# Sinkhorn attention with a bilinear feed-forward: batch 0's q in full width during Sinkhorn

## The chip, the cores and the metric

The kernel runs on one core of one Trainium2 chip. The metric is the device time of one execution in microseconds (us); before the change the median of 7 runs is 251.01 us (250.98 to 251.25). The engines are named as in the profile: PE (matrix multiply; PEld its weight loads), DVE (vector), ACT (scalar), POOL (GpSimd, which also issues the loads from memory), SP (issues the other DMAs).

## The reference

Inputs are q, k, v of 4 batches x 8 heads x 768 positions x 64 and an 8 x 8 `sort_net` per head; the weights `w_a`, `w_b` are 512 x 1536 and `w_out` 1536 x 512. All are float32.

```python
P = sort_net                                  # Sinkhorn, 5 rounds
for _ in range(5):
    P = np.exp(P - P.max(-1, keepdims=True))
    P = P / (P.sum(-1, keepdims=True) + 1e-9)
    P = P / (P.sum(-2, keepdims=True) + 1e-9)
k_sorted = einsum('bhij,bhjcd->bhicd', P, k_blocks)   # 8 blocks of 96 rows
v_sorted = einsum('bhij,bhjcd->bhicd', P, v_blocks)
attn = softmax(q_block @ k_sorted_block.T / 8)        # block by block
x = (attn @ v_sorted), heads side by side             # 3072 x 512
out = ((x @ w_a) * (x @ w_b)) @ w_out
```

## The kernel before, in words

**Layout.** Position `6 p + c` of a sequence lies on partition `p` (128 of them) in chunk `c` (6 of them), so one block of 96 positions is 16 partitions times 6 chunks. Heads are worked in pairs `hp` (0 to 3); `g` counts pairs over all batches. Everything is cast to bf16 as it is loaded. Mixing k or v by the Sinkhorn weights is a matmul of the loaded tile with `s_all`, the weights spread over a block's columns; its result comes out with the head dimension on the partitions. q has to be turned to the same orientation, which is done on PE by a transpose against `ident`.

**Loads.** POOL issues the loads in the order of the program: the first half of batch 0's q (`q_first`), the identity's mask, k and v of the four pairs of batch 0, the first quarter-megabytes of `w_a` and `w_b` (`load_ab(0)`), the second half of `q_first`, `load_ab(1)`. Then comes POOL's share of the Sinkhorn stage (`replicate(nc.gpsimd, 1)`, L445), and behind it `load_ab(2)`, `load_ab(3)`, a spread of the weights (`spread(nc.gpsimd, p_col, 0, 8, ...)`, L470), and the loads for later.

**Sinkhorn, 0 to 12 us.** Five rounds on 32 partitions alternate between ACT (the exponential, L412) and DVE (sums, reciprocals, products). PE meanwhile runs dummy matmuls (`keep_busy`) and, in rounds 3 and 4, four blocks of `half_q(0, hp, "act")`: 12 transposes each, of the 64 partitions that hold the first half of batch 0, copied out of PSUM by ACT. DVE and POOL then replicate the result, half each; `to_columns(0)` and `to_columns(1)` bring the halves to PE's layout. PE and POOL execute their lists strictly in the written order; ACT and DVE do so up to the end of the next stage.

**First half of batch 0, 12 to 22 us.** Mix k and v, scores, exponential, transposes of v (`half_v`), product (`half_o`) and transposes of the result into `xT` (`half_x`), pair by pair, for the first 384 positions. Then five accumulations of the feed-forward are begun (`begun`: three in psF, two in the two banks of one psA tile `two`).

**First feed-forward pass, 24 to 47 us.** Twelve steps `ffn_ab(0, m, 0)`, one for each 128 columns of `w_a` and `w_b`: matmuls into two PSUM banks (L343), a cast by ACT (L363), a product by DVE (L364). Between the steps, `interleave` puts units of the second half of batch 0: Q (`half_q(1, hp, "dve")`, 12 transposes, copied out by DVE), M (mix k and v, both copied out by ACT), R (scores, exponential, transposes of v), o (product) and x (transposes into `xT`). With 20 units, `interleave(steps, units_half(), 1, 3)` runs one unit behind each of the first three steps and then keeps to `ceil((s + 1) * units / 11)`.

**The rest, 47 to 249 us.** The second pass for batch 0, then for each batch two halves of `ffn_ab` and six output blocks `ffn_out` (L386), with the attention of the next batch between them (`units_full`). Batch 1's q is turned on PE by `turn_q` (L271); the q of batches 2 and 3 is turned by DMA.

PSUM is held in two pools: psA (2 buffers of two banks) for scores, products and the full-width mixes, psF (4 buffers of one bank) for everything else.

Of the kernel before, what the change touches and what calls it, by code (L numbers as in the profile page):

```python
# [10 lines left out]
BF16 = mybir.dt.bfloat16  # L11
# [11 lines left out]
def kernel(  # L23
# [54 lines left out]

    q_first = const.tile([P, H, W], BF16, name="q_first")

    def load_q_half(h):
        nc.gpsimd.dma_start(out=q_first[h * PH:(h + 1) * PH],
                            in_=_ap(q, h * PH * W, [[W, PH], [S * D, H], [1, W]]))

    loaded = {}

# [24 lines left out]
            out=w_out_sb[:, c * 4:(c + 1) * 4, :],  # L111
            in_=moe_w_out.rearrange("(kc p) n -> p kc n", p=P)[:, c * 4:(c + 1) * 4, :])

    load_q_half(0)
    make_identity(nc, ident, nomemset=True)
    for hp in range(HP):
        load_pair(0, hp)
    load_ab(0)
    load_q_half(1)
    load_ab(1)  # L120


# [45 lines left out]
                             start=True, stop=True)  # L168


    def half_q(h, hp, eng):
        q_ps = psF.tile([P, NCH, PH], BF16, tag="F", name="q_ps")
        rows = slice(h * PH, (h + 1) * PH)
        for c in range(NCH):
            for e in range(2):
                nc.tensor.matmul(q_ps[e * D:(e + 1) * D, c, :],
                                 lhsT=q_first[rows, 2 * hp + e, c * D:(c + 1) * D],
                                 rhs=ident[rows, rows], is_transpose=True)
        qT = qtp.tile([P, NB, NCH, CG], BF16, tag="qT", name="qT")
        copy(eng, qT[:, 0:NBH].rearrange("p i c t -> p c i t"),  # L180
             q_ps.rearrange("p c (i t) -> p c i t", i=NBH))
        st["q", h, hp] = qT

    def half_mix(h, hp, what, eng, fill=0, cols=512):
        g = h * HP + hp
        src2 = loaded[hp][0 if what == "k" else 1]
# [13 lines left out]

    def half_scores(h, hp):
        g = h * HP + hp
        kT, qT, eT = kTs[g % NBUF], st["q", h, hp], eTs[g % NBUF]
        sc = psA.tile([P, 2, 512], FP32, tag="A", name="sc")
        for i in range(NBH):
            for e in range(2):
                nc.tensor.matmul(  # L207
                    sc[:, e, i * BLK:(i + 1) * BLK],
                    lhsT=kT[e * D:(e + 1) * D, i * BLK:i * BLK + P],
                    rhs=qT[e * D:(e + 1) * D, i], start=True, stop=True)  # L210
        nc.scalar.activation(out=eT[:, 0, :, 0:HB], in_=sc[0:BLK, :, 0:HB],  # L211
                             func=AF.Exp, scale=float(scale))

# [49 lines left out]
        nc.sync.dma_start_transpose(out=qT, in_=st[g, "qc"].rearrange("p c e d -> p (c e d)"))  # L263
        st[g, "qT"] = qT

    def turn_q(g):
        q2 = loaded[g][2]
        q_ps = psF.tile([P, NCH, P], BF16, tag="F", name="q_ps")
        for c in range(NCH):
            for e in range(2):  # L270
                nc.tensor.matmul(q_ps[e * D:(e + 1) * D, c, :],  # L271
                                 lhsT=q2[:, e, c * D:(c + 1) * D],
                                 rhs=ident, is_transpose=True)
        qT = qtp.tile([P, NCH, P], BF16, tag="qT", name="qT")
        nc.vector.tensor_copy(out=qT, in_=q_ps)
        st[g, "qT"] = qT

    def turn_v(g):
# [123 lines left out]
    with tc.manual_schedule(engines={ET.PE, ET.Pool, ET.SP}):  # L402
        with tc.manual_schedule(engines={ET.Activation, ET.DVE}):
            rsum = const.tile([BH, NB], FP32, name="rsum")
            csum = const.tile([BH, NB], FP32, name="csum")
            p_fin = const.tile([BH, NB * NB], FP32, name="p_fin")
            p_rep = const.tile([BH, NB * NB, CG // 2], FP32, name="p_rep")
            pc_ps = psA.tile([P, NB, BH], FP32, tag="A", name="pc_ps")
            heat = psA.tile([P, 2, 512], FP32, tag="A", name="heat")
            keep_busy(heat[:, 0], 8)  # L410
            for it in range(5):
                nc.scalar.activation(out=p_nat, in_=p_nat, func=AF.Exp)  # L412
                if it == 3:
                    half_q(0, 0, "act")
                    half_q(0, 1, "act")
                if it == 4:
                    half_q(0, 2, "act")
                    half_q(0, 3, "act")
                if it == 2:
                    with nc.allow_low_precision("sum of one one and zeros"):  # L420
                        nc.vector.reduce_sum(
                            out=mask, in_=_ap(ident, 0, [[P, P], [1, CG], [CG, NB]]),
                            axis=AX.X)
                nc.vector.reduce_sum(out=rsum, in_=p_nat, axis=AX.X)
                nc.vector.reciprocal(out=rsum, in_=rsum)
                if it > 0:
                    nc.tensor.matmul(heat[0:NB, 1, 0:NB], lhsT=rsum, rhs=rsum,
                                     start=True, stop=True)
                    keep_busy(heat[:, 0], (0, 4, 3, 2, 4)[it])
                nc.vector.tensor_mul(out=p_nat, in0=p_nat,  # L430
                                     in1=_ap(rsum, 0, [[NB, BH], [1, NB], [0, NB]]))
                nc.vector.reduce_sum(out=csum, in_=p_nat.transpose([0, 2, 1]), axis=AX.X)
                nc.vector.reciprocal(out=csum, in_=csum)
                if it < 4:
                    nc.vector.tensor_mul(out=p_nat, in0=p_nat,
                                         in1=_ap(csum, 0, [[NB, BH], [0, NB], [1, NB]]))
                else:
                    nc.vector.tensor_mul(
                        out=p_fin.bitcast(BF16).rearrange("h (i j u) -> h i j u", i=NB, j=NB),
                        in0=_ap(p_nat, 0, [[NB * NB, BH], [NB, NB], [1, NB], [0, 2]]),  # L440
                        in1=_ap(csum, 0, [[NB, BH], [0, NB], [1, NB], [0, 2]]))
            NR = NBH * NB

            def replicate(eng, hf):
                eng.tensor_copy(  # L445
                    out=p_rep[:, hf * NR:(hf + 1) * NR],
                    in_=_ap(p_fin, hf * NR, [[NB * NB, BH], [1, NR], [0, CG // 2]]))

            def to_columns(hf):
                for i in range(hf * NBH, (hf + 1) * NBH):  # L450
                    nc.tensor.matmul(
                        pc_ps[:, i, :],
                        lhsT=p_rep[:, i * NB:(i + 1) * NB].bitcast(BF16).rearrange(
                            "h j t -> h (j t)"),
                        rhs=ident[0:BH, 0:BH], start=True, stop=True)

            replicate(nc.vector, 0)
            replicate(nc.gpsimd, 1)
            to_columns(0)
            spread(nc.vector, pc_ps, 0, 2, 0, NBH)  # L460
            spread(nc.vector, pc_ps, 2, 6, 0, NBH)
            load_ab(2)
            load_ab(3)

            half_mix(0, 0, "k", "act", fill=2, cols=256)
            half_mix(0, 0, "v", "dve")
            to_columns(1)
            half_mix(0, 1, "k", "act")
            nc.vector.tensor_copy(out=p_col, in_=pc_ps)
            spread(nc.gpsimd, p_col, 0, 8, NBH, NBH)  # L470
            half_scores(0, 0)
            half_v(0, 0)
            half_mix(0, 1, "v", "dve")
            half_mix(0, 2, "k", "act", fill=1)
            half_o(0, 0)
            half_scores(0, 1)
            half_v(0, 1)
            half_mix(0, 2, "v", "act")
            half_mix(0, 3, "k", "act", fill=1)
            half_x(0, 0, "dve")  # L480
            half_o(0, 1)
            half_scores(0, 2)
            half_v(0, 2)
            half_mix(0, 3, "v", "act", fill=1)
            half_x(0, 1, "dve")
            half_o(0, 2)
            half_scores(0, 3)
            half_v(0, 3)
            half_x(0, 2, "act")
            half_o(0, 3)  # L490
            begun = [psF.tile([P, 512], FP32, tag="F", name="pf") for _ in range(3)]
            two = psA.tile([P, 2, 512], FP32, tag="A", name="two")
            begun += [two[:, 0], two[:, 1]]
            for n, (m, w_sb) in enumerate(((0, w_a_sb), (0, w_b_sb), (1, w_a_sb),
                                           (1, w_b_sb), (2, w_a_sb))):
                if n == 3:
                    half_x(0, 3, "act")
                ab_mms(begun[n], w_sb, 0, m, 0, range(KA - 1))
# [16 lines left out]


        def units_half():
            Q = [lambda hp=hp: half_q(1, hp, "dve") for hp in range(HP)]

            def M(hp):  # L520
                half_mix(1, hp, "k", "act")
                half_mix(1, hp, "v", "act")
# [2 lines left out]
                half_scores(1, hp)  # L525
                half_v(1, hp)

            us = [Q[0], lambda: M(0), Q[1]]
            for hp in range(HP):
                if hp + 1 < HP:  # L530
                    us.append(lambda hp=hp: M(hp + 1))
                us.append(lambda hp=hp: R(hp))
                if hp + 2 < HP:
                    us.append(Q[hp + 2])
                if hp > 0:
                    us.append(lambda hp=hp: half_x(1, hp - 1, "dve"))
                us.append(lambda hp=hp: half_o(1, hp))
# [97 lines left out]
```

The softmax here doesn't subtract the row's maximum and nothing guards it: scores larger than these inputs give would overflow.

## Time and profile before

| | |
|---|---|
| median of 7 runs | 251.01 us (250.98 to 251.25) |
| the profiled execution | 251.03 us |
| its span, first to last instruction | 249.2 us |
| granted clock of PE over the span | 1.000 |
| PE busy | 239.7 us, 96% |
| DVE, ACT, POOL busy | 112.8, 102.9, 59.3 us |
| matmuls of the feed-forward, L343 and L386 | 155.4 and 60.5 us busy |
| data moved from 6 to 62 us | 190 to 207 GB/s in each slice |
| `q_first`: two loads, 384 KB each as bf16 | 4.9 and 9.8 us from issue to landing |

In a timeline a row gives the start and length in us, the engine and line, what it writes and reads with the tile's shape, how many instructions are merged, and in brackets how long the engine had stood idle and who ended the wait. Ends of matmuls are modelled, so distances from start to next start are used for PE. A wait for several things is put down to the one that came last.

### The profile page before, as it was taken

To read this page: it belongs to the slowest core of one execution; us is meant where nothing else is said; L and a number is where in the kernel's file an instruction comes from. 1 tells how busy PE (TensorE), PEld (TensorE's weight loads), DVE (VectorE), ACT (ScalarE), POOL (GpSimd) and SP (SyncE) were. 2 spreads that over 40 slices of the span, in tenths; PEclk is the share of its full clock that TensorE was granted. 3 is DMA by queue.
4 is the path that set the end of the run, shared out by engine and by line. 5 is a ranking of instruction groups with operands and counts; after the bars stand their busy time and mean duration, and the time that the engine had idled before them with its cause. 6 is when DMAs were issued, how large, how long until landed. Compare 5 with 4: busy or idle time off the path is not lost.

```text
span 249.2 us, 5660 instructions
## 1 busy us (share of the span) xinstructions
PE 239.7 (96%) x2330; PEld 140.0 (56%) x2342; DVE 112.8 (45%) x267; ACT 102.9 (41%) x203; POOL 59.3 (24%) x83
## 2 busy tenths in 40 slices
PE   7889899999999999999999999999999999999994
PEld 2366566666655455666655456666645456665443
DVE  6774546655654323464623334363616144444210
ACT  3365656366633035636343046645440033333001
POOL 8875579449400002305061000000000000000000
PEclk9999999999999999999999999999999999999999
DMA  6999999999832869556475821232134310000132
GB/s 86 190 199 196 197 202 199 207 202 202 100 63 54 169 140 158 88 85 99 77 128 130 202 102 30 45 63 45 33 84 116 119 42 3 0 0 4 42 117 94
DMA packets 49162, 26.85 MB, mean 108 GB/s; under 512 B 25968, under 2 KB 46192, under 8 KB 49136
## 3 DMA queue, kind: packets, MB, share of 16 engines
q0 software_dynamic: 20944, 14.16, 39.2%
q1 hardware_dynamic: 28048, 12.27, 21.1%
q8 instruction: 18, 0.29, 0.5%
q14 instruction: 8, 0.07, 0.1%
q10 hardware_dynamic: 144, 0.07, 0.1%
HBM read 28.32 MB, written 6.29 MB: 139 GB/s over the span
## 4 chain that ended last, share of the span: by engine, by line
PE 90%; DMA 3%; POOL 2%; DVE 2%; issue 1%; ACT 1%; POOLq 0%; DVEq 0%
PE pf L343 50%; PE po L386 24%; PE mix L292 4%; PE o_ps L242 3%; DMA v<-in_v_dram 3%; PE sc L313 2%; PE mixh L192 1%; PE po L373 1%; PE vs_ps L282 1%; PE sc L207 1%; PE vs_ps L219 1%; PE q_ps L271 1%; PE xt_ps L233 1%; DVE hT L364 1%; DVE xph L248 1%
## 5 line engine op out<-in xcount | busy, mean ns | idle before, releaser
L364 DVE TENSOR_TENSOR hT<-a_sb,pf 128x384 bf16<-128x384 bf16 x95 | 52.6, 554 | 73.0 <-PE pf L343 49.1
L343 PE MATMUL pf<-xT,w_a_sb 128*128 128x384 bf16 x380 | 77.9, 326 | 0.0
L343 PE MATMUL pf<-xT,w_b_sb 128*128 128x384 bf16 x380 | 77.5, 326 | 0.0
L363 ACT CAST a_sb<-pf 128x384 bf16<-128x384 f32 x95 | 45.5, 479 | 63.9 <-PE pf L343 42.5
L386 PE MATMUL po<-w_out_sb,hT 128*128 128x512 bf16 x265 | 60.5, 379 | 0.6
L343 PEld LDWEIGHTS <-w_b_sb 128*128 128x128 bf16 x384 | 37.5, 98 | 24.9 <-issue 0.3
L343 PEld LDWEIGHTS <-w_a_sb 128*128 128x128 bf16 x384 | 34.9, 98 | 22.1
L386 PEld LDWEIGHTS <-hT 128*128 128x128 bf16 x276 | 26.4, 98 | 30.2
L161 ACT COPY o_sb<-po 128x512 f32<-128x512 f32 (+1 forms) x13 | 7.5, 578 | 50.5 <-PE po L386 49.1
L163 DVE COPY o_sb<-po 128x512 f32<-128x512 f32 (+1 forms) x12 | 7.9, 659 | 42.5 <-PE po L386 36.9
L318 ACT ACTIVATE eT<-sc 96x768 bf16<-96x768 f32 x24 | 18.1, 803 | 3.2 <-PE sc L313 3.2
L248 DVE TENSOR_TENSOR xp<-o_ps,rec 96x512 bf16<-96x512 f32 x24 | 15.7, 683 | 0.2
L161 ACT CAST kT<-mix 128x384 bf16<-128x384 f32 x24 | 10.3, 482 | 7.9 <-PE mix L292 7.9
L94 POOL DMA_DIRECT2D k<-in_k_dram x16 | 11.5, 721 | 6.7 <-PE pf L343 3.1
L94 POOL DMA_DIRECT2D v<-in_v_dram x16 | 11.5, 717 | 4.3 <-PE pf L343 3.1
L550 POOL COPY gate<-kT 1x1 bf16<-1x1 bf16 x4 | 0.7, 180 | 49.3 <-ACT kT L161 49.3
L242 PEld LDWEIGHTS <-eT 96*128 96x128 bf16 x256 | 10.3, 98 | 3.3 <-ACT eT L211 0.7
L242 PE MATMUL o_ps<-vs,eT 96*128 96x65 bf16 x256 | 11.2, 193 | 0.6 <-ACT eT L211 0.6
L94 POOL DMA_DIRECT2D q<-in_q_dram x12 | 8.6, 716 | 3.2 <-DMA w_out_sb<-in_moe_w_out_dram 1.6
L167 PE MATMUL heat<-warm 128*128 128x512 bf16 x20 | 7.6, 525 | 1.4 <-DVE warm L77 1.3
L257 POOL COPY qc<-q 128x768 bf16<-128x768 bf16 x8 | 6.5, 830 | 5.6 <-DMA q<-in_q_dram 5.6
L211 ACT ACTIVATE eT<-sc 96x768 bf16<-96x768 f32 x8 | 6.5, 808 | 2.9 <-PE sc L207 2.9
(81 smaller groups left out, 162.2 us busy)
## 6 DMA issues: line engine op xcount, KB each, us to landing
out_dram<-o_sb SPq DMA_DIRECT2D x17, 256.0 KB, 2.0
k<-in_k_dram POOLq DMA_DIRECT2D x16, 192.0 KB, 6.7
v<-in_v_dram POOLq DMA_DIRECT2D x16, 192.0 KB, 6.6
q<-in_q_dram POOLq DMA_DIRECT2D x12, 192.0 KB, 7.0
w_a_sb<-in_moe_w_a_dram POOLq DMA_DIRECT2D x6, 256.0 KB, 10.7
w_b_sb<-in_moe_w_b_dram POOLq DMA_DIRECT2D x6, 256.0 KB, 10.4
w_out_sb<-in_moe_w_out_dram POOLq DMA_DIRECT2D x3, 512.0 KB, 10.0
out_dram<-o_sb SPq DMA_DIRECT2D x12, 128.0 KB, 2.4
```

The costliest lines, as they stand in the source:

```text
L94: nc.gpsimd.dma_start(out=to, in_=_ap(t, base, [[W, P], [S * D, 2], [1, W]]))
L161: nc.scalar.copy(out=out, in_=in_)
L163: nc.vector.tensor_copy(out=out, in_=in_)
L167: nc.tensor.matmul(ps[:, 0:cols], lhsT=warm[:, 0:P], rhs=warm[:, 0:cols], start=True, stop=True)
L242: nc.tensor.matmul(o_ps[:, e, i * (D + 1):(i + 1) * (D + 1)], lhsT=eT[:, hf, e, i * BLK:i * BLK + P], rhs=vs[0:BLK, i0 + i, V0 - 1 + e * ( ...
L248: nc.vector.tensor_tensor(out=_ap(xp, i0 * 2 * D, [[nxp * 2 * D, BLK], [D, 2], [2 * D, NBH], [1, D]]), in0=_ap(o_ps, 1, [[1024, BLK], [511 ...
L292: nc.tensor.matmul(mix[e * D:(e + 1) * D, c // 3, c % 3 * P:(c % 3 + 1) * P], lhsT=src2[:, e, c * D:(c + 1) * D], rhs=s_all[:, 2 * g + e], ...
L318: nc.scalar.activation(out=eT[:, hf, :, 0:HB], in_=sc[0:BLK, :, 0:HB], func=AF.Exp, scale=float(scale))
L343: nc.tensor.matmul(pf[:, 0:HW], lhsT=w_sb[:, kc, m * P:(m + 1) * P], rhs=x_cols(b, kc, t), start=(kc == 0), stop=(kc == KA - 1))
L363: nc.scalar.copy(out=a_sb, in_=pf[:, 0:HW])
L364: nc.vector.tensor_mul(out=hT[:, m, t * HW:(t + 1) * HW], in0=a_sb, in1=ab[1][:, 0:HW])
L386: nc.tensor.matmul(po, lhsT=hT[:, m, c * P:(c + 1) * P], rhs=w_out_sb[:, m, :], start=(m == 0), stop=(m == KO - 1))
```

## The change

Batch 0's q is still loaded in two transfers of the same size, but split by heads instead of by partitions: the first holds heads 0 to 3, the second heads 4 to 7, each for all 768 positions. Both are issued ahead of k and v. The four pairs are turned by `turn_q`, which batch 1 uses already: 12 transposes of 128 partitions and a copy of 768 columns, here by ACT. Pair 0 is turned in round 2 of Sinkhorn, pair 1 in round 3, pairs 2 and 3 in round 4. `half_q` goes, and with it the four Q units of the first feed-forward pass, so that `interleave` has 16 units to place instead of 20.

```diff
-    def load_q_half(h):
-        nc.gpsimd.dma_start(out=q_first[h * PH:(h + 1) * PH],
-                            in_=_ap(q, h * PH * W, [[W, PH], [S * D, H], [1, W]]))
+    def load_q(n):
+        heads = slice(n * H // 2, (n + 1) * H // 2)
+        nc.gpsimd.dma_start(out=q_first[:, heads],
+                            in_=_ap(q, heads.start * S * D, [[W, P], [S * D, H // 2], [1, W]]))
...
-    load_q_half(0)
+    load_q(0)
     make_identity(nc, ident, nomemset=True)
+    load_q(1)
     for hp in range(HP):
         load_pair(0, hp)
     load_ab(0)
-    load_q_half(1)
     load_ab(1)
...
-    def half_q(h, hp, eng):
...
     def half_scores(h, hp):
         g = h * HP + hp
-        kT, qT, eT = kTs[g % NBUF], st["q", h, hp], eTs[g % NBUF]
+        kT, qT, eT = kTs[g % NBUF], st[hp, "qT"], eTs[g % NBUF]
...
-                    rhs=qT[e * D:(e + 1) * D, i], start=True, stop=True)
+                    rhs=qT[e * D:(e + 1) * D, :, (h * NBH + i) * CG:(h * NBH + i + 1) * CG],
+                    start=True, stop=True)
...
-    def turn_q(g):
-        q2 = loaded[g][2]
+    def turn_q(g, eng="dve"):
+        q2 = loaded[g][2] if g >= HP else q_first[:, 2 * g:2 * g + 2]
...
-        nc.vector.tensor_copy(out=qT, in_=q_ps)
+        copy(eng, qT, q_ps)
...
                 nc.scalar.activation(out=p_nat, in_=p_nat, func=AF.Exp)
+                if it == 2:
+                    turn_q(0, "act")
                 if it == 3:
-                    half_q(0, 0, "act")
-                    half_q(0, 1, "act")
+                    turn_q(1, "act")
                 if it == 4:
-                    half_q(0, 2, "act")
-                    half_q(0, 3, "act")
+                    turn_q(2, "act")
+                    turn_q(3, "act")
...
-            Q = [lambda hp=hp: half_q(1, hp, "dve") for hp in range(HP)]
-
...
-            us = [Q[0], lambda: M(0), Q[1]]
+            us = [lambda: M(0)]
             for hp in range(HP):
                 if hp + 1 < HP:
                     us.append(lambda hp=hp: M(hp + 1))
                 us.append(lambda hp=hp: R(hp))
-                if hp + 2 < HP:
-                    us.append(Q[hp + 2])
                 if hp > 0:
                     us.append(lambda hp=hp: half_x(1, hp - 1, "dve"))
                 us.append(lambda hp=hp: half_o(1, hp))
```

More of the change, by code (lines that the diff above doesn't have):

```diff
@@ L168, in keep_busy @@
                              start=True, stop=True)
-    def half_q(h, hp, eng):
[L172 to L182, printed above, removed]
     def half_mix(h, hp, what, eng, fill=0, cols=512):
```

## The prediction

> **What bounds the kernel now.** I read the page first, then the chain of waits for the first 26 us, then the timeline of POOL, ACT and PE around the lines the diff touches.
>
> ```profile
> span 249.2 us, 5660 instructions
> ...
> PE 239.7 (96%) x2330; PEld 140.0 (56%) x2342; DVE 112.8 (45%) x267; ACT 102.9 (41%) x203; POOL 59.3 (24%) x83
> ...
> PE 90%; DMA 3%; POOL 2%; DVE 2%; issue 1%; ACT 1%; POOLq 0%; DVEq 0%
> ```
>
> PE carries 90% of the chain, so work taken off PE under the feed-forward counts in full. The other 10% is mostly the start, before PE has anything to do. There the chain reads (start, length, what):
>
> ```profile
> 4.55 6.34 DMA v<-in_v_dram
> 10.89 0.28 issue
> 11.18 0.81 POOL w_a_sb L105
> 11.98 0.15 issue
> 12.13 0.74 POOL w_b_sb L105
> 12.87 0.41 POOL p_rep L445
> 13.29 0.05 issue
> 13.33 0.26 PE pc_ps L451 x4
> ```
>
> The start is set by POOL. Its half of the replication (p_rep, L445) stands in its queue behind the DMA issues, and those wait for earlier loads to land. From 13.33 to 21.9 the same chain is PE, piece after piece, with one DVE stretch of about 1.2 us: what delays 13.33 delays all of it. The timeline of POOL shows the rule of those waits:
>
> ```profile
> 5.27 0.72 POOL L94 DMA_DIRECT2D k<-in_k_dram  x1
> 5.98 0.72 POOL L94 DMA_DIRECT2D v<-in_v_dram  x1
> ...
> 9.14 0.74 POOL L105 DMA_DIRECT2D w_b_sb<-in_moe_w_b_dram  x1 [0.26 <-DMA v<-in_v_dram]
> 10.12 0.70 POOL L82 DMA_DIRECT2D q_first<-in_q_dram  x1 [0.24 <-DMA k<-in_k_dram]
> ```
>
> Numbering POOL's loads from the first q: w_b(0) is the 11th and waits for the 3rd (v of pair 0, landed 8.86), the second q is the 12th and waits for the 4th, w_a(1) is the 13th and waits for the 5th (10.89). Load n is issued about 0.28 after load n-8 has landed. So w_b(1), the 14th, at 12.13, waited for the 6th, k of pair 2, issued 5.27 and landed 6.6 later, 11.84.
>
> On PE, the first feed-forward pass has two stalls next to the units that the change removes:
>
> ```profile
> 25.80 0.38 PE L192 MATMUL mixh<-s_all,v 128*64 128x64 bf16 x12
> ...
> 26.53 0.32 PE L343 MATMUL two<-xT,w_a_sb 128*128 128x384 bf16 x1 [0.36 <-DVE hT L364]
> ...
> 30.25 0.38 PE L176 MATMUL q_ps<-ident,q_first 64*64 64x64 bf16 x12
> ...
> 31.24 0.42 PE L242 MATMUL o_ps<-vs,eT 96*128 96x65 bf16 x8 [0.61 <-ACT eT L211]
> ```
>
> **Part 1: the load order, on the path.** Both versions put 384 KB twice for q, 192 KB each for k and v, and the weights through POOL, 14 loads before p_rep. After, the second q is the 2nd load instead of the 12th, so the 6th is now v of pair 1, and 2 x 384 + 4 x 192 = 1536 KB must have landed for it. Before, 1536 KB (384 + 6 x 192) had landed with v of pair 2: issued 5.98, 6.8 to landing, 12.78. w_b(1) is thus issued at 12.78 + 0.28 = 13.06 instead of 12.13, p_rep starts at 13.80 and PE's second to_columns at about 14.25: **+0.9**. From below: the second q took 1.6 from the landing ahead of it (18.3 to 19.9), against 0.95 for the load of k or v that it displaces: +0.65. From above: between k and v of pair 0 there is one slip of 0.8; half of such a slip more gives +1.3. I take 0.9, from equal bytes at the same moment of the same stream (190 to 199 GB/s in the slices from 6 to 19 us).
>
> The page "DMA: Bandwidth & Descriptors" of the Trainium skill (Anatomy of one DMA) prices a POOL transfer's moving part at bytes / 436 GB/s; an estimate by it for 192 KB more is 0.45, half of the trace's 0.94, and would give 249.7 in place of the time below.
>
> The data are not the limit: k and v land 1 to 2 us later than before, by the byte count k of pair 0 at 9.84, pair 1 at 11.84, pair 2 at 13.76, pair 3 at 15.9; the mixes that read them start at about 12.8, 14.4, 16.0, 17.9. w_a(0) and w_b(0) land by 20.0, needed at 22.6. Behind p_rep on POOL stand load_ab(2), load_ab(3) and the spread (L470, 17.16 before, about 18.1 after, 1.1 long), which the feed-forward's first mix needs only at 25.6. From the 20th load on, the loads landed are the same, so later issues keep their times.
>
> **Part 2: the transposes in Sinkhorn, hidden.** Before, 4 blocks of 12 take 0.19 each on PE. After, 4 of 12 at full width: L271's rows, the same shape, take 0.36 from start to next start (48.44 to 48.80), 1.44 in all. ACT's copies go from 384 to 768 columns: 0.41 to about 0.8 (the 768-column exponential, L211, takes 0.81). The exposed one is the first. It is now queued on ACT between the third and fourth exponential, and PE reaches it only behind the dummy matmuls of iteration 1, at 6.9 (q(0) lands at 6.1). Then 6.9 + 0.55 (0.36 and a matmul's 0.2 to drain) + 0.8 = 8.3 is the earliest fourth exponential, which ran at 7.80:
>
> ```profile
> 7.80 0.26 ACT L412 ACTIVATE p_nat<-p_nat 32x64 f32<-32x64 f32 x1 [1.51 <-DVE p_nat L435]
> ...
> 13.33 0.16 PEld L451 LDWEIGHTS <-p_rep 32*128 32x128 bf16 x4 [0.51 <-POOL p_rep L445]
> ```
>
> That is 0.5 late; the other three copies fit between the exponentials (1.76 apart). DVE's chain and the first two mixes follow 0.5 late, end at 13.35 instead of 12.85, and PE then waits for p_rep until 14.25. Cover: 0.9. So **0**, and up to about 0.4 if the cover is gone (p_rep in time). Scores read qT in strides, as L313 does: its pairs start 0.043 apart, as L207's do: 0.
>
> **Part 3: the feed-forward pass, on the path.** Removed: 4 blocks of half_q, 0.31 from start to next start (25.04 - 24.73, 27.74 - 27.43, 34.41 - 34.10), and around three of them a longer hand-over (0.73 ahead of the second, 0.66 without; 0.33 against 0.23 behind the transposes of v): 4 x 0.31 + 0.26 = **-1.5**. Four DVE copies (0.35) go too, off the path.
>
> The list of units shrinks from 20 to 16, and interleave spreads it anew: M0 after step 0, M1 after step 1, R0 after step 2, then o0, M2, R1 after step 3. So o0 has a whole step (1.3) between it and R0's exponential and its stall (31.24 - 30.56) goes: **-0.68**. The stall at 26.53 (0.44 over the usual 0.29 behind a mix) and 0.12 ahead of M0's v mix go in their present form: **-0.56**.
>
> New waits: M0 now comes directly behind m = 0, when only one psF buffer is free. Its v mix takes begun[0]'s, free when ACT's cast ends (25.16): +0.27. M1 ahead of m = 2 doesn't help that step: its product waits in `two` for DVE's product of m = 1, which needs ACT's cast, now queued behind M0's two copies. ACT: cast to 25.16, kT, vT from 25.63, cast of m = 1 from 26.02 to 26.50; DVE to 27.09; PE is ready at 26.43 and starts at 27.14: +0.71. Together **+0.98**, between +0.2 (the cast goes ahead of the copies, as it did before) and +1.6 (first rival). After that I find the distances one step or more; the 0.2 wait of the last half_x (45.56) stays.
>
> **Sum:** +0.9 + 0 - 1.5 - 0.68 - 0.56 + 0.98 = -0.86. The profiled execution took 251.03 (span 249.2, 1.83 around it), 0.02 above the median of the 7 runs: 251.03 - 0.86 = 250.2 (250.17). Everything behind 47 us only moves earlier: its loads land well ahead (v of batch 1's first pair at 35.2, read at 49).
>
> **The rivals.**
> Buffer order: if psF is handed out in strict turn, M0's mixes get begun[0]'s and begun[1]'s buffers; the v mix waits for DVE (25.75) and m = 2 starts at 27.7: +0.57, **250.7**. For: four buffers, three held. Against: at 24.73 a buffer was had without waiting. 0.20.
> No start delay: if the 13.33 wait doesn't pass on (p_rep not held by the ring), 251.03 - 1.76 = **249.3**. Against: the chain. 0.09.
> Both loads: if the first turn waits for both q loads (the tracking of the tile, not the data), it starts at 8.9, where 768 KB had landed (v of pair 0), the fourth exponential at 10.3, 2.5 late; PE comes to to_columns at 15.3 instead of 14.25. It decides from a turn later than 7.8 on (0.9 of cover behind 6.9). +1.1: **251.3**, slower. Against: half 0 didn't wait for half 1 before. 0.06.
> PE's clock: PE idles 0.9 before to_columns, longer than any of its waits since 7 (0.5). The dummies of 5.2 to 6.4 start 0.427 apart, those from 7.04 0.216: half rate exists here. If that idle brings it back for the next 3.4 us, PE's stretch from 14.25, with hardly a gap, loses up to 1.7: **251.9**, slower. Against: waits of 0.4 to 0.6 passed without. 0.06.
> The page "TensorE: Matmul & The Clock Gate" (Part 1) puts the fall at an idle window of about 3.4 us, which speaks against it; no run shows so long an idle.
>
> **How the numbers follow.** The forecast has 0.59: 250.2, its own range 249.5 to 250.9 from the bounds above. A measurement tells about 0.2%, 0.5 us, from no change. Faster by more: three quarters of the forecast, a third of buffer order, all of no start delay: 0.61. Slower by more: most of the clock, a third of both loads, a little from each other case's tail: 0.09. Within: 0.30. The range for 8 in 10 leaves out no start delay and the clock: 249.4 to 251.2.
>
> **What would show it.** POOL's p_rep at 13.8 and PE's second to_columns at 14.25; the fourth exponential at 8.3; no q_ps between 24 and 47; m = 2 at 26.5 to 27.7 plus 0.9; o0 without a wait; the first pass ending 0.9 earlier. Wrong if p_rep starts below 13.4 or above 14.6, or if the first pass (24.3 to 47.0) shrinks by less than 1.3.

## The result, and the profile after

After takes 248.77 us (median of 13 runs) beside 251.01 before (33 runs): ratio 0.992, interval 0.990 to 0.994, so 2.2 us faster. The profiled execution took 248.77, span 247.0, where before it was 251.03 and 249.2. The forecast of 250.2 had the right sign and four tenths of the size, and 248.77 lies under its range. (In some executions, of unchanged before too, PE's granted clock falls to 0.50 for some microseconds and the time is up to 6 us longer; the ratios leave out executions over 1.5% above the fastest of their kernel, and "level" means those at full clock.)

From the page of after, its span, the busy times by engine and the chain by engine:

```profile
span 247.0 us, 5560 instructions
...
PE 238.3 (96%) x2282; PEld 139.3 (56%) x2294; DVE 111.8 (45%) x263; ACT 104.0 (42%) x203; POOL 59.2 (24%) x83
...
PE 92%; DMA 2%; POOL 2%; DVE 2%; issue 1%; ACT 0%
```

48 matmuls of PE are gone, and 1.4 us of its busy time; the chain is 92% PE instead of 90%. Three stretches of PE's timeline add up to the whole difference:

| stretch of PE | before | after | change | predicted |
|---|---|---|---|---|
| span's start to the last `w_a` matmul of m = 0 | 24.32 | 24.12 | -0.20 | +0.9 |
| from there to batch 1's first q_ps | 24.12 | 22.11 | -2.01 | -1.76 |
| from there to the span's end | 200.8 | 200.8 | 0 | 0 |

The start in the chain of after (start, length, what):

```profile
11.43 0.74 POOL w_a_sb L106
12.18 0.23 issue
12.40 0.74 POOL w_b_sb L106
13.14 0.41 POOL p_rep L435
13.55 0.05 issue
13.60 0.26 PE pc_ps L441 x4
...
18.14 0.31 PE sc L195 x8
```

The wait on POOL is there as before, and to_columns(1) starts at 13.60, 0.27 later than before and not 0.9. And this lateness is gone again five microseconds on. The chain of before shows why, in three lines that the prediction did not use:

```profile
17.87 0.23 PE sc L207 x6
18.10 0.39 issue
18.49 0.22 PE sc L207 x2
```

In the middle of the scores of pair 2 PE stops for 0.39, with nothing that the profile can name as the cause; after has no such stop: its transposes behind these scores start at 18.38, where those of before start at 18.64.

The feed-forward pass, PE's timeline of after:

```profile
24.12 0.33 PE L332 MATMUL pf<-xT,w_a_sb 128*128 128x384 bf16 x1
...
25.02 0.38 PE L180 MATMUL mixh<-s_all,v 128*64 128x64 bf16 x12
...
26.93 0.32 PE L332 MATMUL two<-xT,w_a_sb 128*128 128x384 bf16 x1 [0.61 <-DVE hT L353]
...
29.65 0.41 PE L231 MATMUL o_ps<-vs,eT 96*128 96x65 bf16 x8
...
46.23 0.53 PE L260 MATMUL q_ps<-ident,q 128*64 128x128 bf16 x12
```

The first product of the second half (o_ps, 29.65) starts without a wait, m = 2 waits for DVE at 26.93, and there is no q_ps until batch 1's.

### The profile page after: what moved, and what is told of

Read it like the earlier page. It is cut to its first block, busy times and chain, and to the rows that moved or that the text cites. A ratio compares the mean times of both kernels' runs of the same rounds, so it can differ in the third digit from the quotient of the medians.

```text
span 247.0 us, 5560 instructions
## 1 busy us (share of the span) xinstructions
PE 238.3 (96%) x2282; PEld 139.3 (56%) x2294; DVE 111.8 (45%) x263; ACT 104.0 (42%) x203; POOL 59.2 (24%) x83
## 4 chain that ended last, share of the span: by engine, by line
PE 92%; DMA 2%; POOL 2%; DVE 2%; issue 1%; ACT 0%
PE pf L332 51%; PE po L375 24%; PE mix L281 4%; PE o_ps L231 3%; DMA q_first<-in_q_dram 2%; PE sc L302 2%; PE mixh L180 2%; PE po L362 1%; PE vs_ps L208 1%; PE vs_ps L271 1%; PE sc L195 1%; PE xt_ps L222 1%; PE q_ps L260 1%; POOL w_a_sb L106 1%; POOL w_b_sb L106 1%
```

## The experiments

The theories. As forecast: POOL's replication behind the loads sets PE's start, and what moves p_rep moves everything. The rival that the result brought up: PE stops in the scores of pair 2 until 18.2 to 18.5 in any case, for its own instructions, so that anything that delays or speeds PE ahead of that point counts only beyond it. For the pass: how much is PE's work removed, and how much is the new spacing of the units.

**r_before: before, unchanged, profiled again.**

> The kernel before, unchanged, for a second profile. In the first profile one of the 16 parts of each load landed about 0.4 us behind the other 15 from v of pair 0 on, and PE stood still for 0.39 us at 18.1 us for no reason that the profile shows. Theory A (accidents of that one execution): here k of pair 2 lands near 11.4 instead of 11.84, w_b(1) is issued near 11.7, and the stall at 18.1 is absent or elsewhere. Theory B (they belong to this order of loads): both come again, 11.84 within 0.1 and a stall of 0.3 to 0.5 in the scores of pair 2.

Its time was 250.99, its span again 249.2. POOL's replication, and PE at the scores of pair 2:

```profile
12.29 0.41 POOL L445 COPY p_rep<-p_fin 32x256 f32<-32x256 f32 x1
```

```profile
17.27 0.30 PE L207 MATMUL sc<-qT,kT 64*128 64x96 bf16 x6
18.50 0.22 PE L207 MATMUL sc<-qT,kT 64*128 64x96 bf16 x2 [0.92 <-issue]
```

p_rep is 0.58 earlier than in the first profile of the same kernel (12.87), and nothing comes of it: PE stops 0.53 longer and goes on at 18.50 instead of 18.49. The stop came between the same two matmuls. So the start of the first profile held an accident: k of pair 2, whose landing releases the last issue ahead of p_rep, took 6.6 there and 6.0 here. The records of its 16 parts show 15 landed by 11.39 and one at 11.84 in the first, all 16 by 11.27 here.

**e1_early_load: before, with the second q load moved ahead of k and v, and nothing else.**

```diff
     make_identity(nc, ident, nomemset=True)
+    load_q_half(1)
...
-    load_q_half(1)
```

> The kernel before with the second half of q loaded as the second load, and nothing else changed: the price of the load order alone. By the recorded working (equal bytes): p_rep at 13.8, the first feed-forward pass starts 0.9 later, about 251.9 us. Theory A (as in the changed kernel's trace, the straggling part of a load was an accident): p_rep at 13.1 to 13.2, about 251.3 us against a before with the accident, 251.7 against one without. Theory B (the new order itself frees the start of the straggler and of the stall at 18.1): p_rep at 13.1 and no stall, about 250.8 us, 0.2 below before.

250.72 beside 250.99, ratio 0.9989 (0.998 to 0.9997). p_rep stood at 12.97, 0.68 later than in r_before, as the bytes ahead of it ask. Yet the kernel was no slower. Its scores of pair 2:

```profile
17.90 0.56 PE L207 MATMUL sc<-qT,kT 64*128 64x96 bf16 x8
18.40 0.40 PE L219 MATMUL vs_ps<-ident,vT 128*128 128x128 bf16 x4
```

Eight scores take 0.34 without a stop, so some 0.2 of one is left in these 0.56. The transposes behind them start at 18.40, where they started at 18.65 in r_before. The load order, priced at +0.9, is worth between 0 and -0.3: six of the eleven executions took 250.70 to 250.72 and five 250.96 to 251.08, and unchanged before has executions at both levels.

**e3_prep_first: after, with load_ab(1) behind POOL's share of the replication.**

```diff
-    load_ab(1)
...
+            load_ab(1)
             load_ab(2)
```

> The changed kernel with load_ab(1) issued behind POOL's half of the replication instead of ahead of it. If the start is set by p_rep waiting behind two issues that wait for landings: p_rep runs at about 11.4 to 11.9, PE goes from the first mixes into to_columns(1) at about 12.85 instead of 13.60, and the time falls by about 0.75 to 248.0 us. If the later w_a(1), w_b(1) or k and v of pairs 2 and 3 become the limit, or the start isn't set there: 248.6 to 248.9 us.

248.99, ratio 0.9927 (0.9915 to 0.994): the time of after, within what can be told. p_rep came 1.4 earlier than in after, PE reached the scores 0.4 earlier, and there it stopped:

```profile
11.75 0.51 POOL L434 COPY p_rep<-p_fin 32x256 f32<-32x256 f32 x1 [0.48 <-DVE p_fin L427]
```

```profile
17.66 0.30 PE L194 MATMUL sc<-qT,kT 64*128 64x96 bf16 x6
18.47 0.22 PE L194 MATMUL sc<-qT,kT 64*128 64x96 bf16 x2 [0.51 <-issue]
```

With p_rep out of the way the stop is next, at the same two matmuls and the same time as in before.

**What the stop may be.** Each page lists a queue of instruction transfers (queue, packets, MB, share of 16 engines):

```profile
q8 instruction: 18, 0.29, 0.5%
```

18 packets of 16 KB. In before PE starts 245 of its 4,672 recorded instructions, on average, between one packet's start and the next, so the queue is taken to be PE's. In the records of the packets the first is fetched at 16.0 to 16.1 in before, r_before and after, at 16.2 in e3, and takes 0.97. If PE has used up what it was loaded with, the place of the stop is a number of instructions and its end is the time of the fetch. The page "Runtime: NRT & Kernel Launch" of the Trainium skill (Instruction fetch mechanics) describes such a refill, in blocks of 16 KiB or 256 instructions, and calls it mostly hidden. The block size agrees with the packets; and of the 18 fetches only the first has a stop of PE near it that the profile puts down to "issue", of 0.39 in before and 0.92 in r_before.

**e6_split_dummies: after, with twice as many dummy matmuls of half the width.** 21 more matmuls and as many weight loads ahead of the scores; the dummy columns stay the same.

```diff
-            keep_busy(heat[:, 0], 8)
+            keep_busy(heat[:, 0], 16, 256)
...
-                    keep_busy(heat[:, 0], (0, 4, 3, 2, 4)[it])
+                    keep_busy(heat[:, 0], (0, 8, 6, 4, 8)[it], 256)
```

> The changed kernel with each dummy matmul of the Sinkhorn stage split into two of half the width: the same columns on PE, 42 PE instructions more ahead of the first half of batch 0. New theory (supply): in every run so far in which PE came early to its instruction of the count 446 (the scores of pair 2), it stood there until 18.24 or 18.49 us, whatever p_rep did, so instructions behind that count aren't there before then. If so, the stop moves 42 instructions forward, into the k mix of pair 3 (about 17.4 us), PE stands there for 0.8 to 1.1, and the time rises by that, to 249.5 to 249.9 us. Rival (the stop belongs to the scores of pair 2 or to what they read): no stop at the k mix, 248.7 to 249.0 us.

Neither slower nor faster than after: level 248.7 (median of all twelve 250.13), ratio 0.993 (0.9909 to 0.9951). The times show no stop that moved ahead and cost; the first fetch began at 14.1 instead of 16.0. So more instructions of PE ahead bring the fetch earlier. That form of the supply theory in which the stop comes sooner and lasts as long fell here. And in after an earlier fetch can gain nothing alone, since p_rep sets the same time. Its profile, taken in an execution of 252.6, showed something else, told below.

**e11_before_split: the same edit on before.** Here the theories differ in sign: 21 more matmuls on PE can only cost, unless the supply of instructions is what PE waits for.

> The kernel before with each dummy matmul of Sinkhorn split into two of half the width: 42 PE instructions more, the same columns. Supply theory, second form (the 16 KB fetch of PE's next instructions starts when PE has passed a certain count, and what it brings is there about 2.3 us after its start): with 42 more the count is passed ahead of PE's wait for p_rep, the fetch starts near 14.1 as in e6_split_dummies' profile instead of 16.0, the stop in the scores of pair 2 goes, and more instructions make it faster by 0.3 to 0.5: 250.5 to 250.7 us. Rival (the stop ends at a fixed time, or doesn't come from the fetch): 251.0 us or slower.

250.3 beside 251.02, ratio 0.9957 (0.9931 to 0.9982): faster by 0.7, with more instructions. p_rep is where it was in r_before, the fetch began at 13.4, and the scores ran through:

```profile
12.26 0.41 POOL L445 COPY p_rep<-p_fin 32x256 f32<-32x256 f32 x1
```

```profile
17.19 0.34 PE L207 MATMUL sc<-qT,kT 64*128 64x96 bf16 x8
17.47 0.40 PE L219 MATMUL vs_ps<-ident,vT 128*128 128x128 bf16 x4
```

**e9_prep_split: e3 and e6 together.**

> e3_prep_first (load_ab(1) behind the replication, p_rep at 11.75) with the 42 PE instructions of the split dummies. Second form of the supply theory: no stop at 18.47, so the early p_rep counts: 0.5 to 0.7 less than e3_prep_first, 248.2 to 248.5 us. Rival: the stop stays or moves ahead, 248.9 us or more.

248.25, ratio 0.9877 (0.9841 to 0.9913), beside 248.96 for after on the same chip. The two edits that brought nothing one by one bring 0.7 together, as two limits that end at the same time ask:

```profile
17.37 0.34 PE L194 MATMUL sc<-qT,kT 64*128 64x96 bf16 x8
17.64 0.40 PE L207 MATMUL vs_ps<-ident,vT 128*128 128x128 bf16 x4
```

No stop; the scores start 0.70 ahead of after's 18.07.

**e2_old_spacing: after, with empty units where Q stood.** It keeps the removal of the work and takes back the new spacing.

```diff
+            idle = lambda: None
-            us = [lambda: M(0)]
+            us = [idle, lambda: M(0), idle]
...
+                if hp + 2 < HP:
+                    us.append(idle)
```

> The changed kernel with empty units where the four Q units stood, so that M, R, o and x stand between the steps of the first pass as before: the blocks are gone, the new spacing isn't used. If the new spacing carries a good part of the gain: the product of pair 0 again follows R0 and waits about 1.0 (0.68 and the 0.31 that Q2 filled), the step m = 2 waits about 0.45 to 0.75 instead of 0.61, in all 0.8 to 1.1 slower than the changed kernel, 249.6 to 249.9 us. If the gain is only the removed blocks: no slower than the changed kernel, 248.8 us.

249.8, ratio 0.9964 (0.9947 to 0.9982), 1.1 above after. PE's waits from 13 to 48 us (engine, line, releaser: us in total, times, longest):

```profile
PE o_ps L231 <- ACT eT L200: 0.9, 1, 0.9
PE pc_ps L441 <- POOL p_rep L435: 0.8, 1, 0.8
PE two L332 <- DVE hT L353: 0.6, 1, 0.6
```

The work that Q did between R0 and o0, and ahead of m = 2, had also been cover. Without it those waits grow from 0.61 and 0.36 to 0.92 and 0.64. In after the first is gone, because a whole step of the feed-forward lies between R0 and o0. The second stretch of the table above takes 23.03 here (24.15 to 47.18), 1.09 less than in before and 0.92 more than in after: the pass's 2.0 is about half removal and half spacing.

**e7_r0_early: after, with R0 moved ahead of m = 2.**

```diff
-                want = s + 1 if s < slow else ...
+                want = (1, 3, 3)[s] if s < slow else ...
```

> The changed kernel with R0 (scores and transposes of v of pair 0) put between steps 1 and 2 of the first pass instead of behind step 2. If the wait at m = 2 (0.61 at 26.93) is for DVE's product of m = 1 alone, R0's 0.51 on PE fills it: 0.4 to 0.5 less, 248.3 us. If R0 brings a wait of its own there (a PSUM buffer, or ACT's exponential ahead of the casts): 248.6 to 248.9 us.

248.57 beside 250.98, ratio 0.9912 (0.9897 to 0.9927); lowest 248.12. The stall of m = 2 is gone, the scores and transposes of R0 lie in it:

```profile
27.56 0.34 PE L195 MATMUL sc<-qT,kT 64*128 64x96 bf16 x8
27.84 0.40 PE L208 MATMUL vs_ps<-ident,vT 128*128 128x128 bf16 x4
28.24 0.32 PE L332 MATMUL two<-xT,w_a_sb 128*128 128x384 bf16 x1
```

This profile started late (p_rep at 14.45, with one of the 16 parts of the second q load landed at 9.50 and the others by 8.15), so its times are not to be set beside those of after. The interval overlaps that of after; this run alone does not settle the gain.

**e4_prep_lean: e3, with dummies and small warming matmuls in rounds 1 and 4 alone.**

```diff
-                if it > 0:
+                if it in (1, 4):
...
-                    keep_busy(heat[:, 0], (0, 4, 3, 2, 4)[it])
+                    keep_busy(heat[:, 0], (0, 4, 0, 0, 2)[it])
```

> The kernel with load_ab(1) behind the replication (e3_prep_first), with 7 dummy matmuls and 2 small matmuls of rounds 2 to 4 of Sinkhorn left out, 22 PE instructions fewer ahead of the first half. Supply theory: the stop of 0.51 at 18.47 in e3_prep_first moves 22 instructions back, into the v mix of pair 3, which PE reaches about 0.5 later anyway; the early p_rep now counts, 248.3 to 248.6 us. Rival (the stop belongs to the scores of pair 2): it stays at 18.47, 248.9 to 249.0 us. Should PE's clock fall with fewer dummies, the granted clock shows it and the time is above 249.

Median 252.0, lowest 248.01, ratio 0.9995 (0.9965 to 1.0024). The profiled execution is that lowest one, and even there the clock fell. Windows of it (start and end, length, busy time of PE, PEld, DVE, ACT, POOL, granted clock, DMA share, GB/s):

```profile
5.60:9.00 3.40, 1.48 (x27) 0.80 (x25) 2.74 (x13) 1.98 (x4) 2.54 (x4) 1.00 1.28 196
9.00:12.40 3.40, 3.03 (x37) 1.88 (x40) 2.40 (x11) 1.76 (x3) 2.66 (x5) 0.50 1.31 202
12.40:20.00 7.60, 7.34 (x183) 5.38 (x183) 5.78 (x15) 5.55 (x10) 5.10 (x7) 1.00 1.39 198
```

PE was busy 1.48 of 3.40, and the next 3.40 had half the clock. In ten of the twelve executions the mean granted clock was 0.966 to 0.979, and they took 251.1 to 253.9. The dummies are not free to leave out. For the supply theory the profile speaks all the same: with 22 instructions fewer ahead, the scores of pair 2 run through (17.30, the transposes at 17.58), so the stop of e3 does not belong to them.

**e8_all: e4 and e7 together.**

> e4_prep_lean and e7_r0_early together. If the two gains are of different places they add: about 247.8 us by the supply theory; 248.4 by its rival.

251.6, lowest 249.02, ratio 1.0007 (0.9972 to 1.0043): the same loss, longer, and the gain of e7 can't be seen under it.

```profile
13.20:23.30 10.10, 10.10 (x154) 7.10 (x155) 5.61 (x14) 4.99 (x10) 7.29 (x10) 0.50 1.42 198
```

**e10_prep_split_r0: e9 and e7 together.**

> e9_prep_split with R0 ahead of step m = 2 (as e7_r0_early): another 0.5 less if the two places are separate, 247.7 to 248.0 us; as e9_prep_split if R0 only moves the wait.

247.51 (247.21 to 247.75), ratio 0.9847 (0.9811 to 0.9883), 0.74 below e9 and 1.45 below after on the same chip: faster than both kernels. Here m = 2 follows R0 without a wait:

```profile
25.77 0.34 PE L194 MATMUL sc<-qT,kT 64*128 64x96 bf16 x8
26.05 0.40 PE L207 MATMUL vs_ps<-ident,vT 128*128 128x128 bf16 x4
26.45 0.32 PE L331 MATMUL two<-xT,w_a_sb 128*128 128x384 bf16 x1
```

**r_after: after, unchanged, beside e9 to e11.**

> The changed kernel unchanged, for a second profile and for times on the same chip as the three others: 248.7 to 249.0 us; p_rep between 13.1 and 14.0 by how far the last of the 16 parts of a load lies behind, and no feed-forward step before 24.1.

Ratio 0.9911 (0.988 to 0.9941), median 248.96: the first result again. Its profiled execution was one of 253.69, with half the clock from 14.6 on:

```profile
14.60:28.30 13.70, 13.66 (x160) 9.00 (x159) 6.51 (x15) 5.76 (x10) 8.93 (x12) 0.50 1.44 197
```

## Why the prediction was wrong

**Part 1, the start: the step that failed, twice.** The forecast let "what delays 13.33 delays all of it" stand for the whole start. It left out the "issue" of 0.39 that stood in its own chain at 18.10. That stop ends at 18.2 to 18.5 whatever comes before: r_before 0.58 earlier at p_rep and no faster, e3 0.4 earlier at the scores and no faster, e1 0.68 later at p_rep than r_before and not slower. The sum had to be the later of two: the chain through p_rep, and the stop. With 13.14 for p_rep PE comes to the place of the stop about when the stop ends, and the term is -0.2, not +0.9. The -0.2 is the end of the stop itself: 18.50 in before, gone by 18.25 in e1 and after. Why it ends 0.25 earlier there, no run shows; the times of before lie in steps (250.73, 251.0, 251.25) of this size, so the -0.2 may be chance.

The second error is the base. The price by bytes was nearly right: 13.14 - 12.29 (r_before) is 0.85 beside the forecast 0.93. But it was laid on a profile in which one late part of one load had already cost 0.58. So p_rep came at 13.14, outside the 13.4 to 14.6 that the prediction itself had named.

**Part 2, the transposes in Sinkhorn: 0, as forecast, with some luck in the profile.** The fourth exponential was to come at 8.3, under a cover of 0.9. It came at 7.81, before 7.80. ACT's timeline of after:

```profile
7.12 0.80 ACT L162 COPY qT<-q_ps 128x768 bf16<-128x768 bf16 x1 [0.83 <-PE q_ps L260]
7.81 0.25 ACT L401 ACTIVATE p_nat<-p_nat 32x64 f32<-32x64 f32 x1
```

The copy started at 7.12 instead of the forecast 6.9 + 0.55 = 7.45, and the exponential starts 0.69 behind the start of a copy of 0.80. The cover was not needed here. But the dummy matmuls ahead of the turn took 1.44 in this profile and 1.80 in before's, since the clock became full at 6.03 and 6.76. In e3, where that came at 6.83, PE and ACT show the forecast delay:

```profile
5.06 1.89 PE L167 MATMUL heat<-warm 128*128 128x512 bf16 x4
```

```profile
8.14 0.25 ACT L400 ACTIVATE p_nat<-p_nat 32x64 f32<-32x64 f32 x1
```

The same holds in e7 (8.20) and e10 (8.06). So the mechanism was right, and whether it acts depends on when the clock rises. In e9 and e10, with p_rep early and the stop gone, the chain of the start runs through this turn.

**Part 3, the pass: right in its parts, 0.25 short in the sum.** Removed work, the wait of o0, the order of the units and the new wait of m = 2 are all there. m = 2 starts 2.81 behind m = 0 (forecast 2.82), with a stall of 0.61 on DVE (0.71). The missing 0.25 are small hand-overs: 0.25 instead of 0.34 behind three of the four products where before has it behind one, and 0.09 less at the last half_x. What the sum hid is the weight of its two halves. Removal alone looked like -1.5 and spacing, with its waits gone and come, like -0.26. By e2, removal without spacing gives -1.1, since the waits grow by 0.59 where Q was the cover, and the spacing another -0.9.

**The rivals.** "No start delay" (249.3, chance 0.09) was nearest, and right that the wait does not pass on. Its reason, a p_rep not held by the loads, was wrong: the wait is there and is absorbed behind. The buffer order and both loads did not occur: m = 2 was at 26.93, and the first turn did not wait for the second load. The clock rival (0.06) is not the case of after's median, but it occurs: in r_after's profile PE idles 0.78 ahead of to_columns(1), the clock falls at 14.6, and the execution took 253.69, more than the rival's 251.9. That this idle brings the fall is not shown, since e7's of 1.58 at the same place passed without.

**How 250.17 becomes 248.77.** +0.9 becomes -0.2 (1.1) and -1.76 becomes -2.01 (0.25): 1.35 of the 1.40 between the two; the spans' rounding to 0.1 covers the rest.

## What to carry to other kernels

A step of the chain called "issue" is a term like any other: put it in the sum, and ask what it does to a delay or a gain ahead of it. Where two limits end at the same moment, each edit alone shows nothing; try them together before either is called useless (e3 and e6 gave 0, e9 gave 0.7). And take the base from two profiles of the same kernel when a price hangs on the landing of one transfer.

## What the runs showed of the hardware

- **PE's supply of instructions.** With 21 more, shorter matmuls ahead, before became 0.7 faster, its first instruction fetch began at 13.4 instead of 16.0, and a stop of 0.92 vanished. The stop without them came each time between the same two matmuls, behind 448 recorded instructions of PE (weight loads included) in before, r_before, e1 and e3. That is nearer to two blocks of 256 than to the 2048 instructions that the page "Runtime: NRT & Kernel Launch" of the Trainium skill (Instruction fetch mechanics) gives for PE. Open: what starts the fetch. It lay at 16.0 to 16.2 in before, r_before, after, e1 and e3, although their p_rep stood anywhere from 11.75 to 13.14; PE had begun 338 to 385 recorded instructions by then, but only 258 to 306 at the first fetch of the four runs with split dummies, so no one count sets it. In the four runs with the stop it ends 1.3 to 1.5 before PE goes on. That the fetch ends the stop is inferred from e11 and e9 moving both, not shown by an event.
- **One late part of a load.** A load is released by the last of its 16 parts, and for the loads named above that one was 0.45 behind the rest in the first profile of before and 1.35 in e7's.
- **PE's clock.** In e6's profile PE stood still for 2.09 ahead of to_columns(1), and from 16.0 the clock was 0.50 for 6.8:

```profile
12.90:15.00 2.10, 0.01 (x1) 0.00 (x0) 0.56 (x1) 0.34 (x1) 1.83 (x3) 1.00 1.31 204
16.00:22.80 6.80, 6.80 (x99) 4.42 (x96) 3.82 (x9) 3.85 (x7) 5.55 (x7) 0.50 1.45 196
```

  An idle of 1.58 at the same place in e7's profile passed without, and one of 0.78 in r_after's was followed by 13.7 at 0.50. The page "TensorE: Matmul & The Clock Gate" of the Trainium skill (Part 1) names an idle window of about 3.4 us. The lengths of the half-clock stretches are multiples of that (3.4 in e4, 6.8 in e6, 10.2 in e8, 13.7 in r_after). No idle before them was that long: the longest were 2.09 in e6, 1.96 in e4, 1.33 in e8 and 0.78 in r_after. What decides whether the clock falls stays open.
